# Linear attention into a gated feed-forward: a five-token layout of k and v for five batches, a last tile in three pieces, one copy on another engine, and another split of the first load

## The chip, the cores and the metric

One core of a Trainium2 chip. Its engines each run their own instruction queue in order: TensorE (PE, matmuls; PEld are its weight loads), VectorE (DVE), ScalarE (ACT), GpSimd (POOL) and SyncE (SP, which here only issues DMAs). The metric is the time of one execution on the device in microseconds; lower is better. The kernel before took 327.05 us, the median of three runs (326.86 to 327.49).

## The reference

Cosine-weighted linear attention over 8 batches, 8 heads, 576 positions and a head size of 64, then an RMS norm and a SwiGLU feed-forward (512 to 1536 to 512) over the 4608 tokens. Everything is float32 at the interface.

```python
def _attn_ref(q, k, v) -> np.ndarray:
    B, H, S, D = q.shape
    pos = np.arange(S, dtype=np.float32)
    theta = np.pi / 2.0 * pos / S
    cos_w = np.cos(theta)[None, None, :, None]
    sin_w = np.sin(theta)[None, None, :, None]

    def phi(x, c, s):
        r = np.maximum(x, 0.0)
        return np.concatenate([r * c, r * s], axis=-1)
    q_p = phi(q, cos_w, sin_w)
    k_p = phi(k, cos_w, sin_w)
    kv = np.einsum('bhsf,bhsd->bhfd', k_p, v)
    z = np.sum(k_p, axis=2)
    num = np.einsum('bhsf,bhfd->bhsd', q_p, kv)
    den = np.einsum('bhsf,bhf->bhs', q_p, z)[..., None] + 1e-06
    return (num / den).astype(np.float32)

def _moe_ref(x, w_gate, w_val, w_out, rms_g) -> np.ndarray:
    rms = np.sqrt(np.mean(x * x, axis=-1, keepdims=True) + 1e-06)
    xn = x / rms * rms_g
    g = xn @ w_gate
    silu = g * (1.0 / (1.0 + np.exp(-g)))
    val = xn @ w_val
    return (silu * val @ w_out).astype(np.float32)
```

The sum over positions in `kv` and `z` may be taken in any order, so any assignment of positions to partitions and matmuls gives the same sums.

## The kernel before

The feed-forward runs in nine blocks of 512 tokens: blocks 0 to 7 hold the first 512 positions of each batch, block 8 the last 64 positions ("tails") of all batches; the order is 0, 1, 2, 3, 4, 5, 6, 8, 7. A block has twelve steps (`gval_step`, n = 0 to 11: four gate matmuls and four value matmuls of 128x512 at L446, a Silu on ACT at L466, a product on DVE at L467) and four output tiles (`out_step`, steps 12 to 15: twelve matmuls at L470, a copy to `osb`, a store by SP). The schedule is written out by hand: instructions stand on each engine in the order in which the program emits them, and a table of slots (`at(block, step, "pe" | "mid" | "pre" | "post", ...)`, `run`) says beside which step of the feed-forward the attention work of the next batch is emitted.

The attention work of a batch nb: SP loads k, v and q in two blocks' advance (`load_kv`, L89, `load_q`, L94; batches 1 and 2 by POOL) into a ring of five `raw` buffers. `k_phi` makes the cosine half on DVE (L250) and the sine half on ACT (L248) of `kp`, a `NC` = 9-part tile: a partition holds nine consecutive tokens of one of two heads (64 partitions a head), so that a chunk c has 128 partitions x 4 head pairs x 64. `v_cast` writes v as bf16 beside a column of ones. `kvz_pe` (L317) multiplies them: for each of 4 head pairs, 9 chunks and 2 heads one matmul of 64 rows, 128 columns of weights, 65 moving columns: 72 in all, the two heads of a pair on the two halves of the rows. `kvz_evac` copies the sums. `q_phi`, then a DMA transpose by SP (`q_tr_dma`, L280; for batches 0 and 1 transposes on PE, L297, and a copy, `q_tr_evac`, L242 on ACT or L244 on DVE) make `qpT`; `nd_pe` (L350, 8 matmuls of full rows and 65 columns) makes numerator and denominator of 128 tokens, `nd_post` divides on DVE (`rec` L390 and L393, `xt` L394), `x_sq` on ACT (L406), a power on POOL and `x_norm` on DVE (L416) make the norm, and a DMA transpose by SP (`x_tr_dma`, L430) puts the result into `xnT` of the next block. The kv product of batch nb stands at step 2 of block nb - 1, its k and v work at steps 12 to 15 of the block before, its `nd_pe` at steps 4, 6, 8 and 10.

Batch 1 goes through block 0: its four PE transposes of q stand at steps 9 to 12, with the copies on DVE, and its first `nd_pe` at the beginning of step 12, the second in the middle of that output tile.

The opening handles batch 0 by hand. SP loads its k in two parts, five tokens of each nine and then four (`load_k_tokens`, L110). DVE and ACT make the chunks c = 0 to 8 one after the other; PE runs filler matmuls on each chunk as it is done (`filler_k`, L492), the spread of the norm's weights (`g_spread`, L199) after chunk 3, then the z sums (L328) and the k-v product of batch 0 (L337). `idx_i` holds the token numbers from which the sine and cosine tables `tab` are made: nine columns for k, four for q, one for the tails.

The last output tile of all (block 7, j = 3) is made in two halves of 256 columns, one copied by ACT, one by DVE, each stored by its own DMA:

```python
            for i, bank in enumerate((psC[1], psG[0])):
                cols = (256 * i, 256 * i + 256)
                for m in range(NNT):
                    out_mm(j, m, bank, cols)
                out_store(A if i == 0 else V, blk, j, bank, cols)
```

## Time and profile before

| What | Value |
|---|---|
| three runs | 326.86, 327.05, 327.49 us |
| the profiled execution | 327.27 us, of it 325.5 us span (first to last instruction) |
| granted TensorE clock | 1.00 of full speed |
| L446 matmuls (gate and value) | 379 ns each by modelled ends, 216 ns apart |
| L317 matmuls (k-v products of batches 1 to 7) | 504, busy 9.3 us |
| L350 matmuls (`nd_pe`) | 224, busy 11.4 us |
| `k_phi`, 128x256, mean | DVE 355 ns, ACT 501 ns |
| `q_phi`, 128x512, mean | DVE 494 ns, ACT 714 ns |
| DMA from issue to landing, SP, median | k 7.2, v 6.6, q 8.5 us; stores of 256 KB 2.3 us |

The profile is one execution taken by the hardware profiler. Busy time is given for each engine; a matmul's end is modelled, so the distance between two starts is the better measure of what it costs. A line of a timeline or of the chain has the start in us, the duration, engine, line of the code, and what is written; several like instructions are merged with their number (x8), and idle time before them stands in brackets with what ended it. In the list of waits the three numbers are the sum in us, how often, and the longest. "issue" is time without a visible cause. The chain of waits follows the work back from the last instruction, at each step to what released it. In the rows of DMA issues stand the number, the size and the median us from issue to landing.

### The profile page before, as it was taken

The numbers are of one execution on the slowest core, as the hardware profiler recorded it, in microseconds if no ns is written. First come the engines' busy times: TensorE is split into PE (matmuls) and PEld (weight loads), VectorE is DVE, ScalarE is ACT, GpSimd is POOL, SyncE is SP. The second block draws the span as 40 slices with busy tenths as digits, with TensorE's granted clock in tenths as the row PEclk, the third lists the DMA queues.
The fourth block names the chain that finished last, engine by engine and source line by source line (L and its number), as shares of the span: only waits on it lengthen the run. The fifth ranks groups of instructions, "written<-read, shape, count | busy, mean of one in ns | idle before, by whom it ended". The sixth has DMA issues, their size and how long they took to land.

```text
span 325.5 us, 6461 instructions
## 1 busy us (share of the span) xinstructions
PE 315.7 (97%) x2490; PEld 161.0 (49%) x2527; DVE 182.1 (56%) x390; ACT 169.4 (52%) x343; POOL 40.1 (12%) x76
## 2 busy tenths in 40 slices
PE   7999999999999999999999999999999999999995
PEld 3786555544454445444454445444544444444443
DVE  6676867567737783677557745782577034203410
ACT  4578637854675548546754575446644333223321
POOL 9680301001000100011001000110011000000000
PEclk9999999999999999999999999999999999999999
DMA  7999997889589978994699859964722300050002
GB/s 227 234 271 274 276 337 255 195 180 241 131 175 214 306 122 156 235 297 99 174 205 267 150 145 201 272 155 129 119 51 47 114 34 1 2 110 19 0 34 97
DMA packets 73207, 53.32 MB, mean 164 GB/s; under 512 B 50260, under 2 KB 61784, under 8 KB 73176
## 3 DMA queue, kind: packets, MB, share of 16 engines
q1 hardware_dynamic: 65952, 39.73, 52.7%
q0 software_dynamic: 7216, 13.17, 16.3%
q8 instruction: 20, 0.33, 0.4%
q14 instruction: 11, 0.09, 0.1%
q10 hardware_dynamic: 8, 0.00, 0.0%
HBM read 37.75 MB, written 9.44 MB: 145 GB/s over the span
## 4 chain that ended last, share of the span: by engine, by line
PE 86%; DMA 4%; DVE 4%; ACT 2%; issue 2%; DVEq 0%; ACTq 0%
PE psC L470 26%; PE psV L446 25%; PE psG L446 24%; PE psA L317 2%; PE psA L350 2%; DMA xnT<-xn 2%; DMA raw<-in_k_dram 2%; DVE xt L394 1%; DMA qpT<-qp 1%; DVE xn L416 1%; PE psG L569 1%; PE psV L569 1%; ACT scr L406 1%; PE psC L492 1%; PE psA L569 1%
## 5 line engine op out<-in xcount | busy, mean ns | idle before, releaser
L467 DVE TENSOR_TENSOR hT<-psV,sg 128x512 bf16<-128x512 f32 x104 | 71.6, 689 | 108.4 <-PE psV L446 67.3
L466 ACT ACTIVATE sg<-psG 128x512 f32<-128x512 f32 x104 | 61.5, 591 | 63.6 <-PE psG L446 54.9
L446 PE MATMUL psV<-xnT,wv 128*128 128x512 bf16 x361 | 93.9, 379 | 0.6
L470 PE MATMUL psC<-wo,hT 128*128 128x512 bf16 (+1 forms) x422 | 93.6, 376 | 0.5
L446 PE MATMUL psG<-xnT,wg 128*128 128x512 bf16 x352 | 92.3, 379 | 0.8 <-issue 0.3
L470 PEld LDWEIGHTS <-hT 128*128 128x128 bf16 x444 | 42.7, 98 | 47.3
L446 PEld LDWEIGHTS <-wv 128*128 128x128 bf16 x416 | 40.7, 98 | 49.1
L446 PEld LDWEIGHTS <-wg 128*128 128x128 bf16 x416 | 38.4, 98 | 41.7
L242 ACT COPY osb<-psC 128x512 f32<-128x512 f32 (+1 forms) x36 | 20.8, 579 | 49.9 <-PE psC L470 46.0
L411 POOL TENSOR_TENSOR rs<-ms,mhalf 128x1 f32<-128x1 f32 x36 | 19.8, 550 | 198.1 <-ACT scr L406 198.1
L406 ACT ACTIVATE scr<-xt 128x513 bf16<-128x513 f32 x36 | 22.9, 635 | 23.5 <-DVE xt L394 23.5
L248 ACT ACTIVATE kp<-raw,tab 128x256 bf16<-128x256 f32 x70 | 30.9, 501 | 3.3 <-DMA raw<-in_k_dram 3.3
L416 DVE SCALAR_TENSOR_TENSOR xn<-xt,rs,gb 128x512 bf16<-128x512 f32 x36 | 26.8, 744 | 10.0 <-POOL rs L411 10.0
L394 DVE TENSOR_TENSOR xt<-psA,rec 128x512 f32<-128x512 f32 x36 | 24.9, 691 | 1.2
L248 ACT ACTIVATE qp<-raw,tab 128x512 bf16<-128x512 f32 x32 | 22.6, 714 | 0.5 <-DMA raw<-in_q_dram 0.5
L250 DVE TENSOR_SCALAR kp<-raw,tab 128x256 bf16<-128x256 f32 x74 | 22.0, 355 | 1.3 <-DMA raw<-in_k_dram 1.3
L250 DVE TENSOR_SCALAR qp<-raw,tab 128x512 bf16<-128x512 f32 x31 | 15.1, 494 | 0.0
L350 PEld LDWEIGHTS <-qpT 128*128 128x128 bf16 x224 | 10.5, 97 | 7.1 <-issue 1.0
L446 PE MATMUL psV<-xnT_tail,wv 128*128 128x512 bf16 x48 | 12.3, 379 | 0.1
L446 PE MATMUL psG<-xnT_tail,wg 128*128 128x512 bf16 x46 | 12.0, 379 | 0.1
L350 PE MATMUL psA<-kvzs,qpT 128*128 128x65 bf16 x224 | 11.4, 193 | 0.5 <-DVE xt L394 0.5
L244 DVE CAST vv<-raw 128x1152 bf16<-128x1152 f32 x13 | 9.8, 754 | 0.0
(86 smaller groups left out, 147.9 us busy)
## 6 DMA issues: line engine op xcount, KB each, us to landing
out_dram<-osb SPq DMA_DIRECT2D x31, 256.0 KB, 2.3
raw<-in_k_dram SPq DMA_DIRECT2D x5, 1152.0 KB, 7.2
raw<-in_v_dram SPq DMA_DIRECT2D x5, 1152.0 KB, 6.6
raw<-in_q_dram SPq DMA_DIRECT2D x5, 1024.0 KB, 8.5
raw<-in_k_dram POOLq DMA_DIRECT2D x2, 1152.0 KB, 19.1
raw<-in_v_dram POOLq DMA_DIRECT2D x2, 1152.0 KB, 15.5
raw<-in_q_dram POOLq DMA_DIRECT2D x2, 1024.0 KB, 15.8
wg<-in_moe_w_gate_dram POOLq DMA_DIRECT2D x3, 512.0 KB, 13.9
```

Source lines behind the costliest of these rows:

```text
L242: A.copy(out=o, in_=i)
L248: A.activation(out=out_ap, in_=in_ap, func=AF.Relu, scale=scale)
L250: eng.tensor_scalar(out=out_ap, in0=in_ap, scalar1=scale, scalar2=0.0, op0=ALU.mult, op1=ALU.max)
L350: nc.tensor.matmul(heads[:, g, hp, :], lhsT=qpT[:, h, j * P : (j + 1) * P], rhs=kvzs[b][:, g, hp * E : (hp + 1) * E], start=True, stop=True,)
L394: V.tensor_tensor(out=xt[:, 0:DM].rearrange("p (hp g d) -> p g hp d", g=2, d=D), in0=heads[:, :, :, 0:D], in1=rec[:, :, :].unsqueeze(3).to ...
L406: A.activation(out=scr[:, :], in_=xt[:, 0 : DM + 1], func=AF.Square, scale=1.0 / math.sqrt(DM), accum_out=ms[:, :],)
L411: G.tensor_tensor(out=rs[:, :], in0=ms[:, :], in1=mhalf[:, :], op=ALU.pow)
L416: V.scalar_tensor_tensor(out=xn[:, :], in0=x_of[(b, j)][:, 0:DM], scalar=rs_of[(b, j)][:, :], in1=gb[:, :], op0=ALU.mult, op1=ALU.mult,)
L446: nc.tensor.matmul(bank[:, cols[0] : cols[1]], lhsT=w[:, t, n * P : (n + 1) * P], rhs=x[:, t, cols[0] : cols[1]], start=(t == 0), stop=(t ...
L466: A.activation(out=sg[:, :], in_=g[:, 0:TB], func=AF.Silu)
L467: V.tensor_tensor(out=hT[:, n, :], in0=v[:, 0:TB], in1=sg[:, :], op=ALU.mult)
L470: nc.tensor.matmul(bank[:, 0 : cols[1] - cols[0]], lhsT=hT[:, n, j * P : (j + 1) * P], rhs=wo[:, n, cols[0] : cols[1]], start=(n == 0), st ...
```

## The change

- Batches 3 to 7 hold k and v in another layout. A partition has five consecutive tokens of every head: 576 = 5 x 115 + 1, so 116 partitions are used, and the last of them has one token of its own. Chunk 0 has 116 rows, chunks 1 to 4 have 115 (`rows_of`). The product of a head is five matmuls over all these rows instead of nine over 64; a batch has 40 matmuls instead of 72. `k_phi` has five chunks of 8 heads x 64 instead of nine of 4 x 64, `v_cast` two halves of 116 x 1280. A load of k or v becomes a DMA of 112 rows and one of the 4 rows that are left; for the last batch 3 rows and, in a third DMA, the last token repeated five times, so that nothing past the end is read. `raw` grows to 2560 elements a row, `kp` is one tile with two views, `vv5` is a second tile with its own column of ones.
- The tables get five columns (`idx_i`, `fidx`, `th`, `tab`: 19 and 38 instead of 14 and 28); a minimum keeps token numbers within the sequence.
- The copy of batch 1's fourth q transpose (`q_tr_evac`, j = 3) goes from DVE to ACT.
- Batch 0's k is loaded as four and then five tokens of each nine, both by SP as before, and `g_spread` stands after chunk 4 instead of chunk 3 on PE. The setup of the norm's weights is written at another place; on DVE it stays in the same order.
- The last output tile is made in three pieces: 256 columns (copied by DVE), 128 (ACT) and 128 (DVE), in three banks and with three stores.

The diff, cut to its core:

```diff
@@ -35,6 +35,9 @@
     TB = 512
     HP = H // 2
     NC = S // 64
+    NC5 = 5
+    KP = S // NC5 + 1
+    KM = 112
     NDT = DM // P
     NNT = DFF // P
     E = D + 1
@@ -62,11 +65,25 @@
 
 
 
     def kv_rows(src, b, hps):
         return src[b, 2 * hps[0] : 2 * hps[1], :, :].rearrange(
             "(hp hh) (s c) d -> (hh s) hp (c d)", hh=2, c=NC
         )
 
+    def wide(b):
+        return b > 2
+    def rows_of(c):
+        return KP if c == 0 else KP - 1
+    def kv_rows5(src, b, r0, r1):
+        part = src[b, :, 0 : NC5 * (KP - 1), :].rearrange(
+            "h (p c) d -> p h (c d)", c=NC5
+        )[r0 : min(r1, KP - 1)]
+        return bass.AP(part.tensor, part.offset, [[NC5 * D, r1 - r0]] + list(part.ap)[1:])
     def q_rows(b):
         return q[b, :, 0:512, :].rearrange("h (p j) d -> p h (j d)", j=4)
 
@@ -74,21 +91,34 @@
 
     def raw_tile(which, b):
         if (which, b) not in raw:
-            t = ring.tile([P, HP * NC * D], FP32, name="raw", tag="raw")
+            t = ring.tile([P, H * NC5 * D], FP32, name="raw", tag="raw")
             raw[(which, b)] = t
         return raw[(which, b)]
 
     def raw_kv(which, b):
-        return raw_tile(which, b)[:, :].rearrange("p (hp e) -> p hp e", hp=HP)
+        t = raw_tile(which, b)
+        if wide(b):
+            return t[:, :].rearrange("p (h e) -> p h e", h=H)
+        return t[:, 0 : HP * NC * D].rearrange("p (hp e) -> p hp e", hp=HP)
 
     def raw_q(b):
         return raw_tile("q", b)[:, 0 : H * 4 * D].rearrange("p (h e) -> p h e", h=H)
 
     def load_kv(which, b, hps=(0, HP), eng=nc.sync):
         src = k if which == "k" else v
-        return eng.dma_start(
-            out=raw_kv(which, b)[:, hps[0] : hps[1], :], in_=kv_rows(src, b, hps)
-        )
+        if not wide(b):
+            return eng.dma_start(
+                out=raw_kv(which, b)[:, hps[0] : hps[1], :], in_=kv_rows(src, b, hps)
+            )
+        last = KP if b < B - 1 else KP - 1
+        for r0, r1 in ((0, KM), (KM, last)):
+            eng.dma_start(out=raw_kv(which, b)[r0:r1, :, :], in_=kv_rows5(src, b, r0, r1))
+        if last < KP:
+            eng.dma_start(
+                out=raw_kv(which, b)[last:KP, :, :].rearrange("p h (c d) -> p h c d", d=D),
+                in_=src[b, :, S - 1 : S, :].rearrange("h s d -> s h d").unsqueeze(2)
+                .to_broadcast([1, H, NC5, D]),
+            )
 
     def load_q(b, js=(0, 4), eng=nc.sync):
         return eng.dma_start(
@@ -106,22 +136,21 @@
                 in_=q[2 * pair + i, :, 512:576, :].rearrange("h s d -> s h d"),
             )
 
-    def load_k_tokens(b, c0, c1):
-        return nc.sync.dma_start(
-            out=raw_kv("k", b)[:, :, c0 * D : c1 * D],
-            in_=kv_rows(k, b, (0, HP))[:, :, c0 * D : c1 * D],
-        )
-    load_k_tokens(0, 0, 5)
-    load_k_tokens(0, 5, NC)
     g4 = one.tile([4, P], FP32, name="g4")
     nc.scalar.dma_start(out=g4[:, :], in_=moe_rms_g.rearrange("(t p) -> t p", p=P))
-    idx_i = one.tile([P, 14], mybir.dt.int32, name="idx_i")
+    for c0, c1 in ((0, 4), (4, NC)):
+        nc.sync.dma_start(
+            out=raw_kv("k", 0)[:, :, c0 * D : c1 * D],
+            in_=kv_rows(k, 0, (0, HP))[:, :, c0 * D : c1 * D],
+        )
+    NTAB = 19
+    idx_i = one.tile([P, NTAB], mybir.dt.int32, name="idx_i")
     G.iota(idx_i[:, 0:9], pattern=[[1, 9]], base=0, channel_multiplier=9)
     G.iota(idx_i[:, 9:13], pattern=[[1, 4]], base=0, channel_multiplier=4)
     G.iota(idx_i[:, 13:14], pattern=[[0, 1]], base=512, channel_multiplier=1)
+    G.iota(idx_i[:, 14:NTAB], pattern=[[1, NC5]], base=0, channel_multiplier=NC5)
     warm = one.tile([P, TB], BF16, name="warm")
     V.memset(warm[:, :], 0.0)
     ones = one.tile([P, 1], BF16, name="ones")
...
@@ -202,12 +228,13 @@
                 )
 
     ang = math.pi / 2.0 / float(S)
-    fidx = one.tile([P, 14], FP32, name="fidx")
-    th = one.tile([P, 28], FP32, name="th")
-    tab = one.tile([P, 28], FP32, name="tab")
+    fidx = one.tile([P, NTAB], FP32, name="fidx")
+    th = one.tile([P, 2 * NTAB], FP32, name="th")
+    tab = one.tile([P, 2 * NTAB], FP32, name="tab")
     V.tensor_copy(out=fidx[:, :], in_=idx_i[:, :])
     V.tensor_scalar(
-        out=th[:, 0:14], in0=fidx[:, :], scalar1=ang, scalar2=None, op0=ALU.mult
+        out=th[:, 0:NTAB], in0=fidx[:, :], scalar1=S - 1.0, scalar2=ang,
+        op0=ALU.min, op1=ALU.mult,
     )
     for c0, c1, less in ((0, 9, 576.0), (13, 14, 64.0)):
         V.tensor_scalar(
@@ -215,20 +242,28 @@
             op0=ALU.add, op1=ALU.mult,
         )
     V.tensor_scalar(
-        out=th[:, 14:28], in0=th[:, 0:14], scalar1=math.pi / 2.0, scalar2=math.pi,
-        op0=ALU.add, op1=ALU.min,
+        out=th[:, NTAB : 2 * NTAB], in0=th[:, 0:NTAB], scalar1=math.pi / 2.0,
+        scalar2=math.pi, op0=ALU.add, op1=ALU.min,
     )
     A.activation(out=tab[:, :], in_=th[:, :], func=AF.Sin)
+    V.tensor_copy(
+        out=sel[:, :, :], in_=ident[0:4, 0:4].unsqueeze(2).to_broadcast([4, NDT, P])
+    )
 
     def sin_of(c):
         return tab[:, c : c + 1]
 
     def cos_of(c):
-        return tab[:, 14 + c : 15 + c]
-    kp = one.tile([P, NC, HP, F], BF16, name="kp")
+        return tab[:, NTAB + c : NTAB + c + 1]
+    kp5 = one.tile([P, NC5, H, F], BF16, name="kp")
+    kp = kp5[:, :, :, :].rearrange("p c h f -> p (c h f)")[:, 0 : NC * HP * F].rearrange(
+        "p (c hp f) -> p c hp f", c=NC, f=F
+    )
     vv = one.tile([P, HP, NC, E], BF16, name="vv")
+    vv5 = one.tile([P, H, NC5, E], BF16, name="vv5")
     G.memset(vv[:, :, :, D:E], 1.0)
+    G.memset(vv5[:, :, :, D:E], 1.0)
     qpT = one.tile([P, H, TB], BF16, name="qpT")
     xnT = [one.tile([P, NDT, TB], BF16, name=f"xnT{i}") for i in range(2)]
     xnT_tail = one.tile([P, NDT, TB], BF16, name="xnT_tail")
@@ -255,6 +290,11 @@
     def k_phi(eng, b, c, part, hps=(0, HP)):
         o = slice(0, D) if part == 0 else slice(D, F)
         f = cos_of if part == 0 else sin_of
+        if wide(b):
+            rows = rows_of(c)
+            src = raw_kv("k", b)[0:rows, :, c * D : (c + 1) * D]
+            phi(eng, kp5[0:rows, c, :, o], src, f(14 + c)[0:rows, :])
+            return
         src = raw_kv("k", b)[:, hps[0] : hps[1], c * D : (c + 1) * D]
         phi(eng, kp[:, c, hps[0] : hps[1], o], src, f(c))
 
@@ -301,6 +341,10 @@
         copy(eng, qpT[:, :, j * P : (j + 1) * P], dst)
 
     def v_cast(eng, b, hps=(0, HP)):
+        if wide(b):
+            src = raw_kv("v", b).rearrange("p h (c d) -> p h c d", d=D)
+            hs = slice(2 * hps[0], 2 * hps[1])
+            return copy(eng, vv5[0:KP, hs, :, 0:D], src[0:KP, hs])
         copy(
             eng, vv[:, hps[0] : hps[1], :, 0:D],
             raw_kv("v", b)[:, hps[0] : hps[1], :].rearrange("p hp (c d) -> p hp c d", d=D),
@@ -309,9 +353,16 @@
     heads = psA[:, :, 0 : HP * E].rearrange("p g (hp e) -> p g hp e", e=E)
     kvzs = {}
 
-    def kvz_pe(b, hps=range(HP)):
-        for hp in hps:
-            for c in range(NC):
+    def kvz_pe(b):
+        for hp in range(HP):
+            for c in range(NC5 if wide(b) else 0):
+                for g in range(2):
+                    h, r = 2 * hp + g, rows_of(c)
+                    nc.tensor.matmul(
+                        heads[:, g, hp, :], lhsT=kp5[0:r, c, h, :], rhs=vv5[0:r, h, c, :],
+                        start=(c == 0), stop=(c == NC5 - 1),
+                    )
+            for c in range(0 if wide(b) else NC):
                 for g in range(2):
                     lo, hi = 64 * g, 64 * g + 64
                     nc.tensor.matmul(
@@ -508,7 +559,7 @@
         if c < 7:
             k_phi(A, 0, c, 1)
         filler_k(c)
-        if c == 3:
+        if c == 4:
             g_spread(psC[0])
         if c == 6:
             for i in range(6):
@@ -629,6 +680,7 @@
             f(*args)
 
     KCS = ((0, 1, 2), (3, 4), (5, 6), (7, 8))
+    KCS5 = ((0, 1), (2,), (3,), (4,))
     for c in range(NC):
         at(0, 4 + c // 3, "post", k_phi, V, 1, c, 0)
         at(0, 4 + c // 3, "post", k_phi, A, 1, c, 1)
@@ -637,7 +689,7 @@
         at(0, 7 + j, "post", q_phi, A, 1, j, 1)
         bank = psG[1] if j == 3 else psC[j % 2]
         at(0, 9 + j, "pe", q_tr_pe, 1, j, bank)
-        at(0, 9 + j, "pe" if j == 3 else "pre", q_tr_evac, V, 1, j, bank)
+        at(0, 9 + j, "pe" if j == 3 else "pre", q_tr_evac, A if j == 3 else V, 1, j, bank)
     at(0, 8, "post", load_kv, "k", 2, (0, HP), G)
     at(0, 9, "post", v_cast, G, 1, (0, 2))
     at(0, 10, "pre", v_cast, V, 1, (2, 4))
@@ -668,7 +720,7 @@
     for nb in range(2, B):
         b = nb - 1
         first = nb == 2
-        for i, cs in enumerate(KCS):
+        for i, cs in enumerate(KCS5 if wide(nb) else KCS):
             kb, kn = ((0, 14), (0, 15), (1, 0), (1, 1))[i] if first else (b - 1, 12 + i)
             for c in cs:
                 at(kb, kn, "post", k_phi, V, nb, c, 0)
@@ -726,11 +778,11 @@
         n = 12 + j
         run(blk, n, "pe")
         if blk == last_blk and j == 3:
-            for i, bank in enumerate((psC[1], psG[0])):
-                cols = (256 * i, 256 * i + 256)
+            pieces = ((V, psC[1], 0, 256), (A, psG[0], 256, 384), (V, psG[1], 384, 512))
+            for eng, bank, c0, c1 in pieces:
                 for m in range(NNT):
-                    out_mm(j, m, bank, cols)
-                out_store(A if i == 0 else V, blk, j, bank, cols)
+                    out_mm(j, m, bank, (c0, c1))
+                out_store(eng, blk, j, bank, (c0, c1))
             return
         bank = psC[j % 2]
         for m in range(NNT):
```

More of the change, by code (lines that the diff above doesn't have):

```diff
@@ L154, in load_wo, with g_parts @@
         )
+    g3 = one.tile([4, 3, P], BF16, name="g3")
+    gres = one.tile([4, 2, P], FP32, name="gres")
+    sel = one.tile([4, NDT, P], BF16, name="sel")
+    gb = one.tile([P, DM], FP32, name="gb")
+    def g_parts():
+        rest = g4
+        for i in range(3):
+            V.tensor_copy(out=g3[:, i, :], in_=rest[:, :])
+            if i < 2:
+                V.tensor_tensor(
+                    out=gres[:, i, :], in0=rest[:, :], in1=g3[:, i, :], op=ALU.subtract
+                )
+                rest = gres[:, i, :]
     vv0 = one.tile([P, HP, NC * D], BF16, name="vv0")
@@ L175 @@
     load_w(wg, moe_w_gate, 8, NNT)
-    g3 = one.tile([4, 3, P], BF16, name="g3")
-    gres = one.tile([4, 2, P], FP32, name="gres")
-    sel = one.tile([4, NDT, P], BF16, name="sel")
-    gb = one.tile([P, DM], FP32, name="gb")
-    def g_parts():
-        V.tensor_copy(
-            out=sel[:, :, :], in_=ident[0:4, 0:4].unsqueeze(2).to_broadcast([4, NDT, P])
-        )
-        rest = g4
-        for i in range(3):
-            V.tensor_copy(out=g3[:, i, :], in_=rest[:, :])
-            if i < 2:
-                V.tensor_tensor(
-                    out=gres[:, i, :], in0=rest[:, :], in1=g3[:, i, :], op=ALU.subtract
-                )
-                rest = gres[:, i, :]
     def g_spread(bank):
@@ L310 @@
     kvzs = {}
[L312 to L314 removed]
+    def kvz_pe(b):
[6 more added lines that the diff above has]
+                        start=(c == 0), stop=(c == NC5 - 1),
+                    )
+            for c in range(0 if wide(b) else NC):
                 for g in range(2):
```

## The prediction

> **What bounds the kernel now.** I read the page's first rows, then who waited for whom on the matrix engine (PE), then the chain of waits in order of time, then timelines of the four places that the change touches.
>
> ```profile
> PE 315.7 (97%) x2490; PEld 161.0 (49%) x2527; DVE 182.1 (56%) x390; ACT 169.4 (52%) x343; POOL 40.1 (12%) x76
> ...
> PE 86%; DMA 4%; DVE 4%; ACT 2%; issue 2%; DVEq 0%; ACTq 0%
> ```
>
> PE is busy for 97% and makes 86% of the chain. Beside its very start (1.2 us) it waits three times for longer than 0.3 us:
>
> ```profile
> PE psC L492 <- DVE kp L250: 1.1, 1, 1.1
> PE psG L569 <- ACT xnT L242: 0.7, 1, 0.7
> PE psA L350 <- DVE xt L394: 0.5, 1, 0.5
> ```
>
> These lie at 5, 18 and 46 us. From 50 us to the last matmul no wait for another engine is listed. So time comes only from fewer PE nanoseconds, from the wait at 46 us, or from the two ends; what DVE, ACT or a queue saves between counts for nothing until it makes PE wait.
>
> **Part 1: batches 3 to 7, PE.** A narrow k-v product is 72 matmuls on 64 rows each. The chain around batch 4's:
>
> ```profile
> 93.14 0.86 PE psV L446 x4
> 94.00 1.27 PE psA L317 x72
> 95.27 0.32 PE psG L446
> 95.59 0.05 issue
> 95.64 0.59 PE psG L446 x2
> 96.24 0.86 PE psV L446 x4
> ...
> 98.83 0.24 PE psA L350 x8
> ```
>
> From 94.00 to 96.24 there are 72 L317 and four L446 matmuls (0.86): the product costs 1.38 us. Its single starts say how: pairs start 32 ns apart (36 pairs, 1.15), and entering and leaving the 64-row form costs 0.10 more on each side than the regular spacing. The new product is 40 matmuls on 116 or 115 rows, 65 columns each. The nearest row is L350: full rows, 65 columns, new weights each time, 0.24 us for eight, 30.5 ns by single starts, with no step at either side. 40 x 30.5 ns = 1.22 us. Gain 0.16 a batch, five batches: **-0.80 us**. That 116 rows run in the full form I take from L365 (96 rows, starts 29 ns apart, no step around it). Bounds: 29 ns each gives -1.1; L569 (128 columns, 16 in 0.89 us, 56 ns) is the far bound, 2.23 us a product, +4.3 in all.
>
> [...] The pairs here do start 4 ns apart, but pair follows pair at 32 ns, and the two steps of 0.10 us are paid once a product.
>
> **Part 1, what lies beside PE.** DVE's k work a batch goes from 9 x 355 ns to 5 x 494 ns (128x512 rows of L250), its two v casts from 754 to about 838 ns (1280/1152 elements); ACT from 9 x 501 to 5 x 714 ns. That is 0.6 and 0.9 us less on engines that are 56% and 52% busy and that PE does not wait for here: 0.
>
> The loads are the risk. One was 512 packets of 2304 bytes; it becomes 928 of 1280 bytes and a second, small DMA (a third for batch 7). SP's median k, v and q loads land 7.2, 6.6 and 8.5 us after issue; q is the nearest row in packets (1024 of 1024 bytes). So a wide load takes between nothing and 1.9 us (8.5 - 6.6) longer. By the trace's packet records (93 ns median for 2304 bytes, 55 for 1280) an engine's share goes from 32 x 93 = 3.0 to 58 x 55 = 3.2 us; with the small DMA I take +0.5. Each further issue costs SP about 0.5 us (load issues are 0.39 to 1.49). Queued behind them on SP are the transposes of q (L280) and xn (L430), and nd_pe waits for the former. Smallest slack: in block 1 the first qpT transpose, behind batch 3's k load (issued 58.23, landed 65.73), lands at 66.66, and its reader L350 starts at 68.69: 2.0 us. In block 2 the fourth lands at 105.90 for 109.75: 3.8. xnT of the next block lands at 117.92 for 124.45: 6.5. The loads themselves land 7 to 12 us before k_phi, v_cast and q_phi read them. All of it covers +0.5 + 0.5: **0**. From 2.0 us on, PE pays every microsecond.
>
> [...]
>
> **Part 2: one q copy from DVE to ACT.** DVE at 44 us:
>
> ```profile
> 43.81 0.69 DVE L467 TENSOR_TENSOR hT<-psV,sg 128x512 bf16<-128x512 f32 x1 [2.10 <-PE psV L446]
> 44.42 0.68 DVE L244 COPY qpT<-psG 128x1024 bf16<-128x1024 bf16 x1
> 45.02 0.16 DVE L390 TENSOR_SCALAR rec<-psA 128x8 f32<-128x8 f32 x1
> 45.21 0.20 DVE L393 RECIPROCAL rec<-rec 128x8 f32<-128x8 f32 x1
> 45.45 0.69 DVE L394 TENSOR_TENSOR xt<-psA,rec 128x512 f32<-128x512 f32 x1
> ```
>
> The first nd_pe of batch 1 is done at 44.40, but its rec waits behind the copy. Without it rec starts 0.60 earlier, xt ends at 45.54 instead of 46.14, and the second nd_pe can start at 45.59 instead of 46.19. The six L470 matmuls ahead of it (from 44.23, 216 ns apart) end at 45.53: the wait shrinks from 0.66 (0.50 on the page, which counts modelled ends) to 0.06. Next late would be the third nd_pe, 1.62 after the second by the same DVE work; it moves along. On ACT the copy takes 1.02 us (its two 128x1024 rows), from 44.05 to 45.07, where ACT sits idle from 43.48 to 46.23; behind it waits x_sq, which now starts at 45.6, and the reader of this copy comes at 50.87. **-0.60 us**, bounds -0.50 and -0.66.
>
> **Part 3: batch 0's k.**
>
> ```profile
> raw<-in_k_dram SPq DMA_DIRECT2D x1, 640.0 KB, 5.0
> ...
> raw<-in_k_dram SPq DMA_DIRECT2D x1, 512.0 KB, 6.0
> ```
>
> Issued at 0.72 and 1.23, they land at 5.68 and 7.26: the last 512 KB take 1.58, so 640 KB take 1.98. With the small part first, the first landing comes at 5.28, and the second, after the same 1152 KB, again at 7.26. But chunk c = 4 now hangs on the second. DVE can start it at 7.36 (0.10 after the landing, as 5.78 after 5.68); before it started at 7.09. From a chunk's start to PE's filler matmul on it are 0.44 us at the first chunk, up to 0.62 for a chunk of 0.56 (every other one while POOL issues loads). So PE gets to it at 7.80 to 7.98, and g_spread, which stood ahead of it, now stands behind it.
>
> ```profile
> 7.53 0.84 PE L199 MATMUL psC<-g,sel 4*128 4x128 bf16 x12
> 8.30 0.83 PE L492 MATMUL psC<-kp,warm 128*128 128x256 bf16 x6
> 9.06 0.75 PE L328 MATMUL psA<-ones,kp 64*128 64x1 bf16 x48
> ```
>
> g_spread starts 0.31 after the filler (two of 0.11, a step of 0.09) at 8.11 to 8.29 instead of 7.53, with two fillers (0.22) fewer after it: L328 comes 0.36 to 0.54 late. PE runs dense from there to 12.92 and nothing absorbs it; the loads that it meets next landed 2 us or more early. I take **+0.42 us**; bounds 0 (the second part, now in larger packets beside POOL's loads, lands 0.4 earlier) and +0.65 (it lands 0.1 later). The fourth iota (0.12, as the others), the wider tables and the second memset (0.26) lie in DVE's 1.33 idle us before the first chunk and in POOL's 2.0 before its q_phi; q's landing moves by 0.1, ahead of a PE that is later by more: 0.
>
> **Part 4: last tile.** Before, the last 256 columns on PE (1.31 us) are followed by DVE's copy (321.88, 0.42), the store's issue (322.33) and its landing (324.27, 1.94 after). Two pieces of 128 columns cost 24 x 56 ns, 0.02 more. The copy shrinks by about 0.11 (ACT's 512 and 256 columns take 0.58 and 0.37), the landing by 0.19, half the step from a 512-column store (2.31) to this one. The middle piece is issued by 321.9, ahead of the last at 322.2. **-0.25 us**, bounds +0.05 and -0.50.
>
> **Sum.** -0.80 - 0.60 + 0.42 - 0.25 = -1.23. The profiled execution took 327.27 us, 325.5 of it span; it becomes 326.0. It lay 0.22 above the median of 327.05 shown, to which the same difference gives **325.8 us**. With all good bounds -2.26 (324.8), with the bad ones (products -0.5, opening +0.65, copy -0.5, tail 0) -0.35 (326.7).
>
> **The rivals.** *The transposes are held up.* If wide loads take 4.9 us longer (as long again as a 2304-byte load's packets take, 4.3 to 4.9), block 1 stalls by 4.9 - 2.0 = 2.9 and block 2 by 1.1; later blocks have 5.7 or more: 325.8 + 4.0 = 329.8. It decides from 2.0 us on. For it: transposes land right behind loads on this queue, and DMA is the busiest in these blocks. Against it: 1024-packet q loads need only 4.5 to 5.4. *The full-row product is no cheaper.* At 34.5 ns a matmul the gain is gone: 326.6, and with the bad end of part 3, 326.9, no change; at 56 ns, 330.9. For it: no instruction here has 115 rows. Against: L350 and L365. *The opening loses all of 0.65 and the tail gives nothing:* 325.8 + 0.23 + 0.25 = 326.3; it alone does not change the sign.
>
> **How the numbers follow.** Forecast 0.72, held-up transposes 0.09, product no cheaper 0.10, opening and tail 0.09. 0.2% (0.65 us) is about what a measurement of this kernel tells from no change, so faster means below 326.4. The forecast puts 0.62 below, 0.09 within, 0.01 above; the opening case 0.07 and 0.02; the product case 0.02, 0.05 and 0.03; held-up transposes 0.09 above: 0.71, 0.16, 0.13. The forecast's own range is 324.8 to 326.7; taking in the no-change end of the product case it becomes 324.8 to 327.1.
>
> **What would show it.** Right: L317's successor as 40 matmuls in about 1.2 us with L446 following at once; no L350 wait at 46 us; PE's wait before the fifth chunk's filler at 7.8; the last landing 0.25 sooner after the last matmul. Wrong: PE waits on qpT or xnT in blocks 1 to 5, k-v matmuls 34 ns or more apart, or a second k part that lands well off 7.26.

## The result and the profile after

| | us |
|---|---|
| changed kernel, 6 runs | 325.34 median (324.88 to 326.11) |
| kernel before, 6 runs beside them | 327.04 median (326.77 to 327.8) |
| ratio, 95% interval | 0.9946 (0.9928 to 0.9964) |
| predicted | 325.8, range 324.8 to 327.1 |

The kernel became 1.70 us faster, and the interval lies wholly below 1. The prediction had 1.23 in four terms. The sum came close; two of its terms did not.

The changed kernel was profiled twice: in the first of the runs above (326.11 us, span 324.3), and again among the experiments (324.95 us, span 323.16). First the page of the first profile, its busy row, the clock row in 40 slices and the chain by engine:

```profile
PE 318.5 (98%) x2379; PEld 162.9 (50%) x2379; DVE 181.1 (56%) x370; ACT 167.8 (52%) x324; POOL 40.8 (13%) x78
...
PEclk9799999999999999999999999999999999999999
...
PE 96%; DVE 1%; DMA 1%; ACT 0%; POOL 0%; issue 0%; DVEq 0%; ACTq 0%
```

PE has fewer instructions than before. (Its busy time doesn't compare: before's row has 37 matmuls fewer than the 2527 weight loads, records that are missing; here there are 2379 of each.) The second slice (8.1 to 16.2 us) has a 7 in the clock row. The view by windows shows the stretch (columns: window, its length, busy time of PE, PEld, DVE, ACT and POOL, the granted clock, DMA share and GB/s):

```profile
5.00:10.60 5.60, 4.86 (x108) 3.50 (x108) 4.80 (x13) 4.50 (x10) 5.53 (x11) 1.00 1.14 274
10.60:14.10 3.50, 3.50 (x87) 3.10 (x85) 1.38 (x2) 0.12 (x1) 1.96 (x4) 0.51 1.16 241
14.10:20.00 5.90, 5.17 (x67) 3.25 (x66) 3.97 (x9) 4.99 (x10) 3.73 (x6) 1.00 1.24 206
```

The same windows of the second profile:

```profile
5.00:10.60 5.60, 5.50 (x110) 3.72 (x109) 4.79 (x13) 4.50 (x10) 5.53 (x11) 1.00 1.14 274
10.60:14.10 3.50, 3.34 (x101) 2.57 (x100) 1.61 (x4) 1.55 (x3) 1.97 (x4) 1.00 1.16 238
14.10:20.00 5.90, 4.70 (x75) 3.57 (x75) 4.14 (x9) 4.71 (x10) 4.30 (x6) 1.00 1.24 207
```

In the first, TensorE had half its clock from 10.65 to 14.06 us and got through 87 matmuls where the second did 101. Up to there the two agree within 0.02 us; from there the first is 1.15 us behind to the end. The kernel before has such runs as well: a mean clock of 0.995 or less stands beside 4 of its 55 runs in the experiments and beside 2 of the changed kernel's 12. So the second profile is the one to set beside the profile before, whose clock was full throughout.

Where PE waits for another engine, in the first profile:

```profile
PE psC L543 <- DVE kp L285: 0.8, 1, 0.8
PE psG L620 <- ACT xnT L277: 0.5, 1, 0.5
PE psA L410 <- DVE xt L445: 0.2, 1, 0.2
```

(L401 is now what L350 was, L361 the wide product, L497 the gate and value matmuls, L521 the output matmuls, L285/L283 the halves of `k_phi`, L543 the fillers on the chunks, L225 `g_spread`, L379 the z sums, L620 the first matmuls of block 0.) The wait at 46 us is gone, and no transpose (qpT, xnT) and no load takes its place. The product of batch 4 in the chain of waits, same profile:

```profile
93.40 0.86 PE psV L497 x4
94.27 1.23 PE psA L361 x40
95.50 0.86 PE psG L497 x4
```

Forty matmuls, 1.23 us, with L497 at once behind them. Its groups, and the DVE half of `k_phi`, keeping shapes apart:

```profile
L285 DVE TENSOR_SCALAR kp<-raw,tab 115x512 bf16<-115x512 f32 x20 | 9.3, 480 | 0.0
...
L361 PE MATMUL psA<-vv,kp 115*128 115x65 bf16 x160 | 6.7, 193 | 0.0
```

And the loads by SP, from the rows of DMA issues:

```profile
raw<-in_k_dram SPq DMA_DIRECT2D x5, 1120.0 KB, 7.9
raw<-in_v_dram SPq DMA_DIRECT2D x5, 1120.0 KB, 8.3
raw<-in_q_dram SPq DMA_DIRECT2D x5, 1024.0 KB, 9.5
```

They land 0.7, 1.7 and 1.0 us later after their issue than before (7.2, 6.6 and 8.5). By the trace's packet records a wide load's 928 packets take 4.7 to 6.1 us where 512 took 4.2 to 5.1 (once 3.3), and nobody waited for it.

How the changed kernel (second profile) stands against before, landmark by landmark along PE:

| Up to | this stretch | sum |
|---|---|---|
| first matmul of block 0, at 19 us | -0.31 | -0.31 |
| second `nd_pe` of batch 1, 46 us | -0.57 | -0.88 |
| the five wide products, about 0.14 each | -0.70 | -1.58 |
| start of the last matmul | +0.08 | -1.50 |
| end | -0.84 | -2.34 |

The spans differ by 2.34 us (325.5 to 323.16), the medians by 1.70: the changed kernel's runs spread from 324.67 to 326.35, and this profile lies at their lower end, while that of before had the latest k landing of all (see the opening).

### The profile page after: what moved, and what is told of

Its sections match the earlier page's. It is cut to its first block, busy times and chain, and to the rows that moved or that the text cites. A ratio compares the mean times of both kernels' runs of the same rounds, so it can differ in the third digit from the quotient of the medians.

```text
span 324.3 us, 6183 instructions
## 1 busy us (share of the span) xinstructions
PE 318.5 (98%) x2379; PEld 162.9 (50%) x2379; DVE 181.1 (56%) x370; ACT 167.8 (52%) x324; POOL 40.8 (13%) x78
## 3 DMA queue, kind: packets, MB, share of 16 engines
q0 software_dynamic: 7216, 13.17, 16.4%
## 4 chain that ended last, share of the span: by engine, by line
PE 96%; DVE 1%; DMA 1%; ACT 0%; POOL 0%; issue 0%; DVEq 0%; ACTq 0%
PE psC L521 28%; PE psG L497 28%; PE psV L497 28%; PE psA L401 2%; PE psA L361 2%; DMA raw<-in_k_dram 1%; PE psG L620 1%; PE psV L620 1%; PE psA L368 1%; DVE kp L285 1%; PE psA L388 1%; PE psG L337 1%; PE psA L620 1%; PE psA L426 0%; PE psC L543 0%; PE psG L521 0%
## 5 line engine op out<-in xcount | busy, mean ns | idle before, releaser
L521 PE MATMUL psC<-wo,hT 128*128 128x512 bf16 (+1 forms) x432 | 94.4, 376 | 0.0
L497 PE MATMUL psV<-xnT,wv 128*128 128x512 bf16 x368 | 94.4, 379 | 0.0
L497 PE MATMUL psG<-xnT,wg 128*128 128x512 bf16 x368 | 94.4, 379 | 0.0
L521 PEld LDWEIGHTS <-hT 128*128 128x128 bf16 x456 | 42.9, 98 | 47.3
L497 PEld LDWEIGHTS <-wv 128*128 128x128 bf16 x416 | 40.7, 98 | 49.1
L497 PEld LDWEIGHTS <-wg 128*128 128x128 bf16 x416 | 38.5, 98 | 41.4
L277 ACT COPY osb<-psC 128x512 f32<-128x512 f32 x35 | 20.5, 586 | 51.0 <-PE psC L521 51.0
L283 ACT ACTIVATE kp<-raw,tab 128x256 bf16<-128x256 f32 (+2 forms) x50 | 28.4, 609 | 2.2 <-DMA raw<-in_k_dram 2.2
L283 ACT ACTIVATE qp<-raw,tab 128x512 bf16<-128x512 f32 x32 | 22.6, 714 | 0.5 <-DMA raw<-in_q_dram 0.5
L285 DVE TENSOR_SCALAR kp<-raw,tab 128x256 bf16<-128x256 f32 (+2 forms) x54 | 20.8, 431 | 0.2 <-DMA raw<-in_k_dram 0.2
L285 DVE TENSOR_SCALAR qp<-raw,tab 128x512 bf16<-128x512 f32 x31 | 14.7, 478 | 0.0
L401 PEld LDWEIGHTS <-qpT 128*128 128x128 bf16 x224 | 10.5, 97 | 6.5 <-issue 0.4
L497 PE MATMUL psG<-xnT_tail,wg 128*128 128x512 bf16 x48 | 12.3, 379 | 0.0
L497 PE MATMUL psV<-xnT_tail,wv 128*128 128x512 bf16 x48 | 12.3, 379 | 0.0
L401 PE MATMUL psA<-kvzs,qpT 128*128 128x65 bf16 x224 | 11.4, 193 | 0.0
L279 DVE CAST vv<-raw 116x1280 bf16<-116x1280 f32 (+1 forms) x13 | 10.5, 806 | 0.0
```

Source lines behind the costliest of these rows:

```text
L277: A.copy(out=o, in_=i)
L283: A.activation(out=out_ap, in_=in_ap, func=AF.Relu, scale=scale)
L285: eng.tensor_scalar(out=out_ap, in0=in_ap, scalar1=scale, scalar2=0.0, op0=ALU.mult, op1=ALU.max)
L401: nc.tensor.matmul(heads[:, g, hp, :], lhsT=qpT[:, h, j * P : (j + 1) * P], rhs=kvzs[b][:, g, hp * E : (hp + 1) * E], start=True, stop=True,)
L497: nc.tensor.matmul(bank[:, cols[0] : cols[1]], lhsT=w[:, t, n * P : (n + 1) * P], rhs=x[:, t, cols[0] : cols[1]], start=(t == 0), stop=(t ...
L521: nc.tensor.matmul(bank[:, 0 : cols[1] - cols[0]], lhsT=hT[:, n, j * P : (j + 1) * P], rhs=wo[:, n, cols[0] : cols[1]], start=(n == 0), st ...
```

## The experiments

"Wide" is the five-token layout. The kernel before, run beside the experiments, had medians of 326.99 (e1 to e4), 327.26 (e5 to e8) and 327.0 us (e9 to e11).

### One part at a time

**e1: batch 0's k as four and five tokens, alone.**

```diff
-    load_k_tokens(0, 0, 5)
-    load_k_tokens(0, 5, NC)
+    load_k_tokens(0, 0, 4)
+    load_k_tokens(0, 4, NC)
...
-        if c == 3:
+        if c == 4:
             g_spread(psC[0])
```

> Part 3 alone on the kernel before: batch 0's k as four and five tokens, the spread after chunk 4. The prediction's theory: the second landing stays at 7.26 us, PE waits for the fifth chunk, +0.42 us (0 to +0.65). The rival, read from the changed kernel's profile: the second part lands near 6.4, the z sums start 0.4 earlier, -0.4 us; and where the granted clock falls to half for 3.4 us from about 10.6 on, +0.8 instead.

Measured: 327.25 us (326.67 to 327.71, 11 runs), ratio 0.9998 (0.9984 to 1.0013): no change. In its profile the z sums start at 8.70 us (before 9.06), so the opening gained 0.36 rather than lost 0.42. The gain went again at 35 us, in this profile, which is of the slowest of the eleven runs. The list of PE's waits, with one that before doesn't have, and its place in ACT's timeline:

```profile
PE psC L297 <- ACT qp L248: 0.6, 1, 0.6
```

```profile
35.30 0.72 ACT L248 ACTIVATE qp<-raw,tab 128x512 bf16<-128x512 f32 x1 [1.77 <-DMA raw<-in_q_dram]
```

ACT stood idle for 1.77 us until batch 1's q, loaded by POOL, landed at 35.28; PE's transposes wait for what ACT makes of it. This landing lies between 34.2 and 35.3 us in the eight profiles with POOL's loads in their old order in which an engine waits for it, whatever PE gained: a floor that PE reaches when it is early and the load is late.

**e2: the wide layout alone** (the changed kernel with the old split, the old place of `g_spread`, the copy on DVE and the tail in two halves).

```diff
-    for c0, c1 in ((0, 4), (4, NC)):
+    for c0, c1 in ((0, 5), (5, NC)):
...
-        if c == 4:
+        if c == 3:
             g_spread(psC[0])
...
-        at(0, 9 + j, "pe" if j == 3 else "pre", q_tr_evac, A if j == 3 else V, 1, j, bank)
+        at(0, 9 + j, "pe" if j == 3 else "pre", q_tr_evac, V, 1, j, bank)
...
-            pieces = ((V, psC[1], 0, 256), (A, psG[0], 256, 384), (V, psG[1], 384, 512))
-            for eng, bank, c0, c1 in pieces:
+            for i, bank in enumerate((psC[1], psG[0])):
+                cols = (256 * i, 256 * i + 256)
                 for m in range(NNT):
-                    out_mm(j, m, bank, (c0, c1))
-                out_store(eng, blk, j, bank, (c0, c1))
+                    out_mm(j, m, bank, cols)
+                out_store(A if i == 0 else V, blk, j, bank, cols)
```

> Part 1 alone (five-token layout for batches 3 to 7, with the wider tables). Theory: each of the five products 0.14 to 0.16 us shorter, -0.7 to -0.8 us, no PE wait on a transpose. Rival (transposes held up by the longer loads): above 0, PE waits on qpT or xnT in blocks 1 to 5. Its first load is split five and four as before, so it is also a second sample of when that lands: 5.7 and 7.3 us if the split decides, anything from 6.4 on if it varies from run to run.

Measured: 325.89 us (325.64 to 326.48, 5 runs), ratio 0.9965 (0.9952 to 0.9977). Chain of waits around batch 4's product in its profile, and from PE's waits the old one at 46 us, still there:

```profile
93.70 1.23 PE psA L361 x40
```

```profile
PE psA L401 <- DVE xt L445: 0.5, 1, 0.5
```

The products give 0.70 here too. Another 0.36 appears where this kernel has no edit at all: from the last matmul's start to the end it takes 3.62 us, before 3.98. The tail's table below takes that up.

**e3: the copy of the fourth q transpose on ACT, alone.**

```diff
-        at(0, 9 + j, "pe" if j == 3 else "pre", q_tr_evac, V, 1, j, bank)
+        at(0, 9 + j, "pe" if j == 3 else "pre", q_tr_evac, A if j == 3 else V, 1, j, bank)
```

> Part 2 alone (the fourth q copy of batch 1 on ACT). Theory: the wait of 0.66 us at 46 us falls to 0.06 to 0.09, -0.6 us for good. Rival: the gain is given back at the next wait, 0.

Measured: 326.51 us (326.21 to 327.12, 11 runs), ratio 0.9984 (0.9974 to 0.9994). Its list of waits has no L350 line; the 0.57 us won at 46 us is kept to the end. In the changed kernel the place looks like this (PE's timeline, then ACT's, second profile):

```profile
43.69 0.41 PE L401 MATMUL psA<-kvzs,qpT 128*128 128x65 bf16 x8
43.93 1.46 PE L521 MATMUL psC<-wo,hT 128*128 128x512 bf16 x6
45.31 0.40 PE L401 MATMUL psA<-kvzs,qpT 128*128 128x65 bf16 x8
```

```profile
43.89 1.01 ACT L277 COPY qpT<-psG 128x1024 bf16<-128x1024 bf16 x1 [0.71 <-PE psG L337]
45.35 0.63 ACT L457 ACTIVATE scr<-xt 128x513 bf16<-128x513 f32 x1 [0.45 <-DVE xt L445]
```

The second `nd_pe` now starts 0.09 us after the six L521 matmuls are through, where 0.66 were lost before, and the copy fills idle time of ACT: behind it ACT still has 0.45 us to wait for DVE.

**e4: the last tile in three pieces, alone.**

```diff
-            for i, bank in enumerate((psC[1], psG[0])):
-                cols = (256 * i, 256 * i + 256)
+            pieces = ((V, psC[1], 0, 256), (A, psG[0], 256, 384), (V, psG[1], 384, 512))
+            for eng, bank, c0, c1 in pieces:
                 for m in range(NNT):
-                    out_mm(j, m, bank, cols)
-                out_store(A if i == 0 else V, blk, j, bank, cols)
+                    out_mm(j, m, bank, (c0, c1))
+                out_store(eng, blk, j, bank, (c0, c1))
```

> Part 4 alone (last tile in three pieces). The prediction: -0.25 us (+0.05 to -0.50). Rival, read from the changed kernel's profile: last matmul to end of span 3.1 instead of 3.9 us, -0.8 us, of which 0.3 is the number of semaphore waits that SP still has to go through after the last landing (one instead of six).

Measured: 326.65 us (326.33 to 327.8, 11 runs), ratio 0.9989 (0.998 to 0.9998); from the last matmul's start to the end 3.41 us, 0.58 less than before. The four parts alone give +0.26 - 1.10 - 0.48 - 0.34 = -1.66 us by their medians: they add up to what the change gives together.

### The tail: why part 1 shows in it

Before's tail and the changed kernel's (second profile) in the timeline of all engines:

```profile
320.32 1.47 PE L470 MATMUL psG<-wo,hT 128*128 128x256 bf16 x12
320.52 0.37 ACT L242 COPY osb<-psC 128x256 f32<-128x256 f32 x1 [0.72 <-PE psC L470]
321.88 0.42 DVE L244 COPY osb<-psG 128x256 f32<-128x256 f32 x1 [9.68 <-PE psG L470]
```

```profile
318.74 1.50 PE L521 MATMUL psG<-wo,hT 128*128 128x128 bf16 x24
...
319.65 0.27 ACT L277 COPY osb<-psG 128x128 f32<-128x128 f32 x1 [1.44 <-PE psG L521]
320.28 0.29 DVE L279 COPY osb<-psG 128x128 f32<-128x128 f32 x1 [0.86 <-PE psG L521]
```

What follows is SP's: it issues the last store and then goes through a row of waits on semaphores, one of which is the landing of that store. By the trace's records of these waits:

| | before | changed | difference |
|---|---|---|---|
| last matmul's start to the last copy's start | 0.37 | 0.26 | -0.11 |
| last copy | 0.42 | 0.29 | -0.13 |
| store's issue to the end of the wait on its landing | 1.98 | 1.70 | -0.28 |
| from there to the end | 1.19 | 0.87 | -0.32 |

The last row is the surprise. Each of these closing waits takes some 0.06 us even when it is met long before. Before, three stand ahead of the landing's and five behind it (324.38 to 324.62); in the changed kernel none stands behind, all are passed while SP waits anyway. e2 has one behind (3.62 us from the last matmul's start to the end), e1 and e3 five (3.97 and 3.98), e4 four (3.41). Five of them at 0.06 us are 0.3 us, and before, e1, e2 and e3 have the same stores. What differs between the groups is how many DMAs SP issues. By the trace SP's DMAs take eight semaphores in turn, and the closing waits go through these in a fixed order; the wide loads' small second parts move the last store to another place in the row. To test this:

**e11: four more DMAs, nothing else** (before, with four of the q tail loads cut in halves).

```diff
-            nc.sync.dma_start(
-                out=rqt[pair][64 * i : 64 * i + 64, :, :],
-                in_=q[2 * pair + i, :, 512:576, :].rearrange("h s d -> s h d"),
-            )
+            for h0, h1 in ((0, 4), (4, H)) if pair > 1 else ((0, H),):
+                nc.sync.dma_start(
+                    out=rqt[pair][64 * i : 64 * i + 64, h0:h1, :],
+                    in_=q[2 * pair + i, h0:h1, 512:576, :].rearrange("h s d -> s h d"),
+                )
```

> The kernel before with the tail loads of q for the last two pairs in halves, so that four more DMAs are issued and nothing else changes. Theory: which of SP's closing semaphore waits the last store's landing holds up goes by the number of DMAs; four more leave one or two waits behind the landing instead of six, and the end comes 0.25 to 0.3 us sooner after the last matmul (3.98 to about 3.7), -0.08%. Rival: six waits behind the landing as before, 3.98 us.

Measured: 326.86 us (326.48 to 329.37, 10 runs), ratio 0.9998 (0.9982 to 1.0015). From the last matmul's start to the end 3.66 us, with one wait behind the landing's instead of five. The row of waits moved as the theory said, and all thirteen profiles fit it: with 122 DMAs on SP (before, e1, e3) five waits stand behind the landing's, with 123 (e4) four, with 125 (e7, below) two, with 126 (e11) and, eight further, 134 (e2) one, with 135 (the changed kernel and the others) none. But 0.3 us in the time of the whole is less than these runs can tell, so the gain is shown in the trace only. (This profile, of the run of 329.37, had the lowered clock, from 8.1 to 14.93 us; the tail lies far behind that.)

### The opening and the scatter

**e5: the changed kernel with part 3 undone.**

```diff
-    for c0, c1 in ((0, 4), (4, NC)):
+    for c0, c1 in ((0, 5), (5, NC)):
...
-        if c == 4:
+        if c == 3:
             g_spread(psC[0])
```

> The changed kernel with part 3 undone (five and four tokens, spread after chunk 3). Floor theory (the opening is bounded at 35 us by the landing of batch 1's q load, which varies from run to run, so part 3 is worth nothing): the same as the changed kernel within its scatter, about 325.3 us, ratio to the kernel before 0.994 to 0.996. Rival 1 (the prediction: part 3 costs 0.42 us): 324.9, 0.9932. Rival 2 (part 3 gains 0.4 us): 325.7, 0.9958 or more.

**e6: the changed kernel, `g_spread` after chunk 3 again**, the second half of the same edit.

```diff
-        if c == 4:
+        if c == 3:
             g_spread(psC[0])
```

> The changed kernel with the spread back after chunk 3, four and five tokens kept. The spread then fills PE while it waits for the fifth chunk: the z sums start up to 0.2 us earlier. Floor theory: no change in the median, 325.3 us. If PE in the opening decides instead: -0.2 us, 325.1.

Measured: e5 324.97 us (324.76 to 326.05, 6 runs), ratio 0.9934 (0.9918 to 0.995); e6 325.01 us (324.71 to 326.37, 6 runs), ratio 0.9935 (0.9917 to 0.9952). Both are the changed kernel's time. By its number alone e5 would fit rival 1 as well (324.9); against that rival stand e6, which keeps the new split, and the changed kernel itself in e10 (324.98). e6's other expectation missed: its z sums start at 8.76, 0.1 us later than in the changed kernel and not up to 0.2 earlier. The two openings by `g_spread` and the start of the z sums, in PE's timeline of e5 and of the second profile of the changed kernel:

```profile
6.91 0.84 PE L225 MATMUL psC<-g,sel 4*128 4x128 bf16 x12
7.68 0.83 PE L543 MATMUL psC<-kp,warm 128*128 128x256 bf16 x6
8.44 0.75 PE L379 MATMUL psA<-ones,kp 64*128 64x1 bf16 x48
```

```profile
7.34 0.84 PE L225 MATMUL psC<-g,sel 4*128 4x128 bf16 x12
8.12 0.61 PE L543 MATMUL psC<-kp,warm 128*128 128x256 bf16 x4
8.66 0.75 PE L379 MATMUL psA<-ones,kp 64*128 64x1 bf16 x48
```

With five tokens first they start at 9.06 (before), 8.59 (e2), 8.80 (e3), 8.80 (e4) and 8.44 (e5), mean 8.74 (e11, whose clock had fallen by then, left out). With four first and `g_spread` after chunk 4 they start at 8.66 to 8.70 in all six profiles. The second part of k is what scatters: the last of its packets ends between 5.81 and 6.63 us with the old split (six profiles) and between 5.86 and 6.16 with the new (seven). The profile of before, on which the prediction's term was built, held the latest of the thirteen.

The trace shows what was late. A part counts as landed at the sixteenth raise of its semaphore: in the changed kernel's first profile these come at 4.60 and 6.41, and ACT starts the first chunk that reads the part at 4.68 and 6.43. In before's profile fourteen of the second part's sixteen raises come by 6.45 us and the last two at 7.13 and 7.26. In e3 and e4, whose openings are the same as before's, fifteen come by 6.38 and 6.45 and the last at 6.59 and 6.62. In the changed kernel the last comes at 6.41 and 6.44 (two profiles). So one opening's landing moves by 0.7 us from run to run, and one or two late raises make up the difference; what delays them is not shown. A rival is left open: with the old split all four kernels built on before land later (6.59 to 7.26) than the two built on the changed kernel (6.39 and 6.46), and with the new split so does e1 (6.65, the others 6.38 to 6.51). Something else in the changed kernel, such as the setup of the norm's weights written at another place, may bring the load forward; no run separates it.

**e8 and e9: is the late q what makes runs differ?** Batch 1's q is loaded earlier on POOL: the last load of the value weights is cut in two and q goes between the halves. In e9 the second half is issued later still, behind the second token tile's power on POOL. The edit of e8:

```diff
-    load_w(wv, moe_w_val, 8, NNT)
+    load_w(wv, moe_w_val, 8, 10)
     load_q(1, eng=G)
+    load_w(wv, moe_w_val, 10, NNT)
```

> The changed kernel with the last load of value weights cut in two and batch 1's q load between the halves, so that it has 256 KB less ahead of it: it lands about 1.3 us earlier (33 instead of 34.3 to 35.3). Floor theory: PE never waits for it at 35 us, the later runs of the scatter go, median 324.9 to 325.0 us against 325.3. Rival (the scatter is the clock's fall or something else): 325.3 as before, no wait at 35 us either way.

The edit of e9:

```diff
-    load_w(wv, moe_w_val, 8, NNT)
+    load_w(wv, moe_w_val, 8, 10)
     load_q(1, eng=G)
...
     x_norm(0, 0)
     x_sq(0, 1)
+    load_w(wv, moe_w_val, 10, NNT)
     load_kv("v", 1, eng=G)
```

> As the kernel with batch 1's q load between two halves of the value weights, but the second half issued after the second norm's power on POOL instead of before it. Theory: the issue of 0.77 us no longer stands ahead of that power, so the new wait of 0.5 us of the transposes on the second x_norm goes; q still lands before 34 us and PE doesn't wait at 35: 324.7 us with runs within 0.2 us. Rival (the narrow scatter of that kernel was its new wait hiding the late loads): 324.7 to 325.9 in its runs, as the changed kernel.

Measured: e8 325.15 us (325.12 to 325.20, 6 runs), ratio 0.9933 (0.9919 to 0.9947). Its q landed at 33.73 us, but PE has a new wait:

```profile
PE psC L487 <- DVE xn L467: 0.4, 1, 0.4
```

POOL's third issue (0.77 us from 17.82) stands ahead of the power at 18.58 that `xn` hangs on. e9 takes that away (no L487 line, q at 33.88, no wait at 35 us) and gives 325.12 us (324.6 to 326.0, 6 runs), ratio 0.9943 (0.9929 to 0.9957). Its six runs scatter as widely as the changed kernel's. So the late q is not the only source of the scatter, as e9's rival had it, and no version here beats the changed kernel clearly.

**e10: the changed kernel again.**

> The changed kernel itself once more, beside the others of this job. Theory: runs from 324.8 on, up to 0.9 us more where batch 1's q load lands late with the clock at full, and about 1.2 us more where the clock falls to half for one window of 3.4 us at about 10.6 us (granted clock 0.995 over the span). Rival: all runs within 0.3 us of each other.

Measured: 324.98 us (324.67 to 326.35, 6 runs), ratio 0.9947 (0.9932 to 0.9961); its profile is the second one used above. Four runs lie between 324.67 and 324.99, one at 326.35 with a clock of 0.995 and one at 325.93 at full clock. The rival (all within 0.3 us) fell; the fall of the clock accounts for one of the two late runs, the other is unexplained.

### The rival with the largest price: transposes held up

**e7: each wide load as one DMA** of 116 rows (batch 7: 115 rows and the last token).

```diff
-        for r0, r1 in ((0, KM), (KM, last)):
+        for r0, r1 in ((0, last),):
```

> The changed kernel with each wide load as one DMA of 116 rows (115 and the last token for batch 7) instead of 112 and the rest. If the number of rows decides on how many DMA engines a load is spread (4 for 116, 5 for 115), a load's packets take about 232 x 55 to 80 ns = 13 to 19 us instead of 5.3, the transposes behind it on SP's queue come 8 to 13 us late, PE waits for qpT in block 1 and later ones, and the kernel is 15 to 50 us slower. If all 16 engines share it whatever the rows: within 0.3 us of the changed kernel.

Measured: 373.85 us (371.82 to 379.06, 4 runs), ratio 1.14 (1.1369 to 1.143). The list of PE's waits:

```profile
PE psG L497 <- DMA xnT<-xn: 19.4, 4, 7.5
PE psA L401 <- DMA qpT<-qp: 13.6, 4, 6.7
```

The 928 packets of a load now take 13.6 to 16.4 us, although one packet takes no longer (median 55 ns; 68 in the changed kernel's first profile): fewer are under way at a time. By these medians 928 x 55 ns are 51 us of packets in 13.6 to 16.4 us, three to four at a time, and 928 x 68 ns are 63 us in 4.7 to 6.1 us, 10 to 13 at a time (estimates). The raises differ with it: as its data lands, a load of 112 rows raises its semaphore sixteen times, one of 116 rows four times, and batch 7's of 115 rows five times (10.0 and 11.2 us). Four packets at a time, as many as the raises, would take 928 x 55 ns / 4 = 12.8 us, near what was measured (estimate). What the raises stand for, and what ties them to the number of rows, is not shown. The transposes of q and xn, queued behind the loads, are late by up to 7.5 us, just as the rival said, and PE waits 33.0 us for them in eight places; the lowered clock (a mean of 0.95) adds to that. So the rival's mechanism exists, and the split at row 112 is what keeps it away.

## Why the prediction came out as it did

- **What bounds the kernel** was right. With PE at 96% of the chain, what came off the products, the wait at 46 us and the tail reached the end (the opening's gain in e1's profile did not: it went again at 35 us), and what DVE and ACT lost or gained did not (`k_phi` 480 and 720 ns, predicted 494 and 714; no wait followed). The parts alone add up to the whole because they lie one behind the other on PE.
- **The products**: mechanism right, size 0.10 too large. Starts lie 30.8 ns apart where 30.5 was taken from L350, and neither entering nor leaving the new product costs a step: 40 x 30.8 ns = 1.23 us, where 1.22 was predicted. The old product measures 1.372, where 1.38 was read. Both differences go the same way: 0.14 and not 0.16 a batch, -0.70 for -0.80. The gain is the two steps alone: 36 pairs at 32.6 ns are 1.17 us, less than the new 1.23, and the steps of 0.095 and 0.10 us come on top. So "the full-row product is no cheaper", which needed 34.5 ns a matmul, fell.
- **The copy**: -0.57 measured, -0.60 predicted, with the wait down to 0.09 (predicted 0.06) and the copy in the idle stretch of ACT that was named.
- **The loads**: wide ones land 0.7 (k) and 1.7 us (v) later after issue, where 0.5 for the load and 0.5 for the second issue were allowed. Of the 0.5 for the load the packets gave 0.2; no run shows the 0.3 taken for the small DMA, and in the first profile the 4-row DMAs of batches 3 to 6 land within 0.05 us of the 112-row ones (batch 3's k at 66.64 and 66.62). Of the 2.0 us of slack in block 1 the second profile has 0.98 left (landing 66.84, `nd_pe` 67.82). Held-up transposes did not occur; e7 shows them when a load takes some 10 us more.
- **The opening failed.** The step that failed is "the second, after the same 1152 KB, again at 7.26". It landed at 6.41, and the first part at 4.60 and not at 5.28. So DVE began the fifth chunk at 6.43 and not at 7.36, PE's filler on it ran at 7.04, `g_spread` started at 7.35, not at 8.11 to 8.29, and the z sums 0.4 us early, not 0.4 late. The sign of being wrong that was named, a second part well off 7.26, is there. One profile's landing was taken for the kernel's landing. Part 3 is worth nothing that can be measured, alone (e1) or within the whole (e5). Its good bound, 0, was the right value.
- **The tail was mis-sized**: -0.84 for -0.25, outside the bounds given (-0.50). Copy and landing together gave -0.41 (predicted -0.30; with the 0.02 for two pieces that is -0.28, not the -0.25 that was taken) and the shorter last matmuls -0.11. The rest, -0.32, is SP's closing waits, which the sum ended before. They are only partly the tail's doing: the pieces alone bring -0.58 (e4), the wide layout alone -0.36 (e2).
- **The total**: with the two failed terms as they turned out, the sum of the prediction would have been -0.80 - 0.60 + 0 - 0.84 = -2.24 in place of -1.23, near the -2.34 of the second profile. The medians show -1.70, the scatter of the changed kernel's runs taking some of it. That 325.34 lies so near 325.8 is in part luck: two errors of the same sign, about 0.4 and 0.6 us, met a median that the scatter had raised.

What stays open: some of the changed kernel's runs take 325.7 to 325.9 us at full clock, others 324.7 to 325.0, and neither the k landing nor the q landing alone explains it; nor is it shown why the k landing differs between kernels.

## What to carry to other kernels

A landing time read from one profile is one draw (the same opening gave 6.59, 6.62 and 7.26 us): where a term hangs on one, bound it by how far such landings move from run to run, or take no gain and no loss from it. Follow the end of a kernel to its very last instruction: what the queue does after the last store has landed is part of the time, and an edit elsewhere can move it. When a load gets another number of rows, look in the trace at how long its packets take together, not only at one packet.

## What the runs showed of the hardware

- TensorE's clock fell to half for 3.41 us (10.65 to 14.06) in one profile of the changed kernel, behind a stretch of fillers and one-column matmuls whose starts lie at most 0.38 us apart (the last longer wait, 0.76 us, ended at 5.55); it cost 1.15 us. e6 shows the same (10.46 to 13.87), e11 a fall of 6.83 us (8.10 to 14.93), twice as long. The second profile has the same stretch and no fall, so the stretch alone is not the cause.
- Two row-packed matmuls of 64 rows with fresh weights take 32.6 ns from pair to pair, one full-row matmul of 65 columns 30.8, and the packed form costs 0.095 us to enter and 0.10 to leave. For these shapes, 36 pairs in a row, packing halves is no gain over full rows once the two steps are counted.
- An 1160 KB load whose outer dimension is 116 rows takes 13.6 to 16.4 us and raises its semaphore four times as data lands; one of 112 and 4 rows takes 4.7 to 6.1, the 112 rows with sixteen raises, the 4 rows with four. Both have 928 packets, of 55 and 68 ns at the median.
- SP's closing waits take 0.06 us each, and how many stand behind the last landing goes down by one with each further DMA of SP and repeats after eight (122 to 135 DMAs here).
